# Per-tile stores in token order, float32 loads of the first tile on the SyncE queue, and decay tables from one position table, in a fused retention and top-k expert kernel

## The chip, the core and the metric

The kernel runs on one core of a Trainium2 chip. The metric is device time in microseconds (us). The engines are TensorE (PE for its matmuls, PEld for its weight loads), VectorE (DVE), ScalarE (ACT), GpSimd (POOL) and SyncE (SP). Each takes its instructions in the order in which the program issues them, and waits on semaphores for the others. DMA transfers are issued by POOL or by SP and run on 16 DMA engines.

## What is computed

Shapes are batch 4, heads 8, sequence 768, head width 64, all float32. First comes a linear attention with a decay per head, then a layer that passes the 128 highest-scored tokens of each batch through a two-layer network and adds the gated result to them; all other tokens keep the attention's output.

```python
gamma = 1.0 - 2.0 ** (-5.0 - np.arange(H))            # attention
for t in range(S):
    state = gamma * state + einsum('bhd,bhe->bhde', k[:, :, t], v[:, :, t])
    y[:, :, t] = scale * einsum('bhd,bhde->bhe', q[:, :, t], state)

x = y.transpose(0, 2, 1, 3).reshape(B, S, 512)        # experts
scores = einsum('bsd,d->bs', x, w_gate)
out = x.copy()
for b in range(B):
    top_idx = np.argpartition(-scores[b], capacity)[:capacity]    # 128 of 768
    ye = np.maximum(x[b, top_idx] @ w1, 0.0) @ w2                 # 512 -> 1024 -> 512
    g = 1.0 / (1.0 + np.exp(-scores[b, top_idx]))
    out[b, top_idx] = x[b, top_idx] + g[:, None] * ye
```

## The kernel before

**Tiles.** The sequence is cut into tiles of 256 tokens, three per batch, twelve in all (j = 0 to 11, batch j // 3). A partition of a loaded tile holds two consecutive tokens (r = 0, 1), so that a load moves runs of 128 elements per head (`tok`, line 294). Each tile is two chunks c of 128 tokens, and heads come in four pairs hp, or in two halves u. The loads of q, k and v (`load`, line 299) are issued by POOL, cast from float32 to bfloat16 on the way, and go to seven rotating buffers each. There are two loads of 128 KB for each tile and tensor, 72 in all; four more load w1 and four w2.

**The order.** All work is cut into small steps, and the string `ORDER` (line 32) is the order in which they are issued, over all engines at once. The number after a step is its tile, chunk or batch; a name such as S6 or P0 is the PSUM bank, or pair of banks, that it uses. Each engine works through its own steps in this order. The steps that matter here:

- `c_*`: constants. `c_iota*` write position tables on POOL; `c_small`, `c_mask`, `c_ident`, `c_late` and others work on DVE; `c_gq` and `c_gk` (lines 261 and 257) are exponentials on ACT that make the decay tables gq and gk for the three tile positions in a batch; `warm` (line 333) is four matmuls on zeros, which compute nothing that is used.
- `l_q`, `l_k`, `l_v`, `l_w1`, `l_w2`: the loads.
- `ks` (line 340): k times its decay table, on DVE. `tq` and `tk`: transposes of q and scaled k on PE. `eq` (times gq, on DVE) and `ek` (on ACT) bring them back from PSUM.
- `qk`, `mk`: products of q and k on PE, and the causal mask on DVE. `kv`, `se`: the state's update on PE, and its copy on ACT. `qs`, `av`: the output from the state and from the masked products.
- `ey` (line 430): the transposed output yT from PSUM, on ACT. `tx`, `ex`: it is transposed into rows and written to xs (bfloat16, all 24 chunks stay). `sp`, `esp`: the scores.
- `srt`, `esr`, `cp`, `cpi`, `dg`, `rk`, `oh`: for each batch the rank of each token by comparison with all others. Equal scores are told apart by the table `tie` on the diagonal blocks. `oh` is a one-hot matrix of the chosen. `spl`, `ga`, `ega`, `sig`: the chosen tokens' index and gate.
- `gx`, `egx`, `m1`, `rl`, `m2`, `cb`: chosen rows are gathered by a matmul, then the two layers and the gate.
- `st` (line 577): a store of rows to the output; `sca` (line 585): a scatter of the 128 results of a batch. For batches 0 to 2 the scatter adds to what the store has written; for batch 3 the row is gathered too (`gr`), added on chip (`cb`, line 562), and the scatter writes plainly. A scatter waits for the stores of its batch. Stores and scatters are issued by POOL, and between two of them POOL writes one element (`spaced`, line 572).

**Order of tokens.** Within a chunk of 128 tokens, the columns of yT, and so the partitions of xs, are ordered by r first and token pair second: partition 64 r + i is token 2 i + r. Each of the eight stores therefore takes one r of one batch: 64 partitions, six chunks, every second row of the output, 768 KB. The tables `lq` and `tie` hold this order.

**Start and end.** The order begins with the constants, eight `warm` steps between them (32 matmuls), and the loads of tile 0. It ends with

```python
"... st 3 1;gr 3 S6; st 3 0;rl 2 2 P1; ... m2 2 2 S6;egx 3 S5;m1 3 0 P0;cb 2 S6;m1 3 1 P0; ..."
"... sca 2;ga 3 S6; m2 3 0 S4;rl 3 1 P0;ega 3 S6;sig 3;m2 3 1 S4;cb 3 S4;sca 3;"
```

so that batch 3's scatter comes last.

Of the kernel before, what the change touches and what calls it, by code (L numbers as in the profile page):

```python
# [15 lines left out]
try:  # L16
# [13 lines left out]
NX = 7  # L30
EKD, EXD = [], []
ORDER = (
    "c_small;c_tab;l_v 0 1;l_wg;l_k 0 1;c_szero;c_iota;c_zero;warm S6;l_k 0 0;c_mask;c_gq 0;warm S6;c_slg;"
    "c_ident;l_k 1 1;warm S6;c_wg;l_k 1 0;warm S6;c_gk 2;c_iota2;warm S6;l_q 0 0;c_gk 1;l_q 0 1;warm S6;c_gq 1;"
    "l_q 1 0;warm S6;c_iota3;warm S6;l_v 0 0;c_late;c_gk 0;l_q 1 1;tq 0 0 S6;c_gq 2;l_v 1 1;eq 0 0 S6;l_k 2 0;"
    "ks 0 1;tq 0 1 S6;ks 0 0;tk 0 1 S0;l_k 2 1;ks 1 2;tk 0 0 S1;ek 0 1 S0;eq 0 1 S6;l_v 1 0;tk 1 2 S2;ek 0 0 S1;"
    "qk 0 1 P2;l_q 2 1;ek 1 2 S2;qk 0 0 P0;mk 0 1 P2;kv 0;l_v 2 1;tq 1 2 S6;se 0;mk 0 0 P0;l_v 3 0;kv 1;l_q 2 0;"
    "se 1;eq 1 2 S6;qs 0 P1;av 0 1 P1;l_v 2 0;av 0 0 P1;qk 1 0 P2;ks 2 2;l_k 4 0;ey 0 P1;qk 1 1 P0;mk 1 0 P2;"
    "tk 2 2 S6;l_k 3 1;kv 2;ek 2 2 S6;l_k 3 0;sp 0 S2;mk 1 1 P0;tx 0 S3;l_q 3 1;se 2;esp 0 S2;ex 0 S3;l_q 5 0;"
    "qs 1 P2;av 1 1 P2;l_k 4 1;kv 3;av 1 0 P2;l_q 3 0;se 3;tq 2 2 S6;ey 1 P2;kv 4;l_q 4 0;eq 2 2 S6;l_v 3 1;"  # L40
    "se 4;qk 2 0 P0;sp 1 S6;qk 2 1 P1;mk 2 0 P0;l_q 4 1;tx 1 S4;l_v 4 1;ex 1 S4;ks 3 2;qs 2 P0;l_v 5 0;"
    "av 2 0 P0;mk 2 1 P1;tk 3 2 S5;l_v 7 1;ek 3 2 S5;esp 1 S6;ks 4 2;av 2 1 P0;l_v 4 0;ey 2 P0;tq 3 2 S6;"
    "l_k 6 0;tk 4 2 S4;eq 3 2 S6;l_q 5 1;tx 2 S5;ek 4 2 S4;sp 2 S6;l_k 5 1;qk 3 0 P1;esp 2 S6;qk 3 1 P0;"
    "mk 3 0 P1;ex 2 S5;kv 6;l_k 5 0;tq 4 2 S6;spl 0;se 6;srt 0 6 P2;mk 3 1 P0;kv 7;esr 0 6 P2;l_k 9 1;qs 3 P1;"
    "eq 4 2 S6;av 3 1 P1;se 7;av 3 0 P1;cp 0 3;l_v 5 1;qk 4 1 P0;qk 4 0 P2;ey 3 P1;cp 0 5;kv 8;l_k 6 1;"
    "mk 4 1 P0;se 8;l_q 6 0;tx 3 S6;sp 3 S2;tq 5 2 S3;ex 3 S6;mk 4 0 P2;l_q 6 1;l_v 6 1;kv 9;eq 5 2 S3;qs 4 P0;"
    "se 9;l_v 6 0;av 4 1 P0;ks 5 2;av 4 0 P0;l_q 9 0;esp 3 S2;cp 0 4;ey 4 P0;tk 5 2 S6;l_k 8 1;kv 10;cp 0 0;"
    "ek 5 2 S6;cp 0 1;tx 4 S4;l_k 9 0;sp 4 S5;ks 6 2;ex 4 S4;l_q 8 0;qk 5 1 P1;qk 5 0 P0;esp 4 S5;cp 0 2;"
    "tk 6 2 S6;l_q 7 1;se 10;mk 5 0 P0;tq 6 2 S5;l_v 8 0;ek 6 2 S6;eq 6 2 S5;l_q 7 0;qs 5 P0;kv 12;mk 5 1 P1;"
    "l_k 7 0;qk 6 0 P2;se 12;av 5 0 P0;l_k 7 1;qk 6 1 P1;mk 6 0 P2;av 5 1 P0;l_q 9 1;kv 13;ey 5 P0;mk 6 1 P1;"  # L50
    "l_q 8 1;qs 6 P2;av 6 0 P2;se 13;sp 5 S6;l_k 8 0;tx 5 S0;ks 9 2;av 6 1 P2;l_q 11 0;ex 5 S0;esp 5 S6;"
    "dg 0 0 6;tk 9 2 S6;spl 1;srt 6 6 P1;ey 6 P2;tq 7 2 S1;l_v 7 0;rk 0 S0;ek 9 2 S6;eq 7 2 S1;l_q 10 0;ks 7 2;"
    "sp 6 S1;esr 6 6 P1;tx 6 S6;l_v 9 0;esp 6 S1;oh 0 S0;tq 9 2 S1;ex 6 S6;tk 7 2 S4;l_v 8 1;eq 9 2 S1;ga 0 S5;"
    "tq 8 2 S6;ek 7 2 S4;l_v 10 1;ega 0 S5;ks 8 2;gx 0 S5;l_k 11 0;sig 0;cp 1 2;l_v 10 0;eq 8 2 S6;qk 7 0 P1;"
    "tk 8 2 S4;l_v 9 1;cp 1 5;egx 0 S5;kv 14;mk 7 0 P1;ek 8 2 S4;l_q 10 1;qk 7 1 P0;l_k 10 1;se 14;mk 7 1 P0;"
    "qk 8 1 P2;qk 8 0 P1;l_w1 0;kv 15;qs 7 P0;mk 8 0 P1;l_k 10 0;se 15;av 7 1 P0;av 7 0 P0;l_v 11 0;kv 16;"
    "cp 1 1;ey 7 P0;qk 9 0 P1;l_w2 1;mk 8 1 P2;l_q 11 1;qk 9 1 P0;se 16;tx 7 S6;mk 9 1 P0;sp 7 S4;l_w1 1;"
    "tq 10 2 S5;ex 7 S6;l_k 11 1;kv 18;eq 10 2 S5;st 0 0;qs 8 P0;cp 1 0;l_w1 2;av 8 1 P0;mk 9 0 P1;se 18;"
    "av 8 0 P0;l_w1 3;ey 8 P0;kv 19;ks 10 2;l_v 11 1;qs 9 P1;av 9 1 P1;se 19;cp 1 3;sp 8 S6;st 1 0;av 9 0 P1;"
    "tx 8 S5;esp 8 S6;dg 1 0 6;l_w2 0;ey 9 P1;kv 20;l_w2 2;tk 10 2 S6;ex 8 S5;sp 9 S0;l_w2 3;tq 11 2 S1;cp 1 4;"  # L60
    "st 0 1;ek 10 2 S6;esp 9 S0;esp 7 S4;tx 9 S0;eq 11 2 S1;st 2 1;srt 12 6 P1;se 20;ks 11 2;st 2 0;qk 10 1 P2;"
    "ex 9 S0;srt 18 2 S6;mk 10 1 P2;rk 1 S1;spl 2;esr 12 6 P1;tk 11 2 S0;oh 1 S1;esr 18 2 S6;qk 10 0 P2;st 1 1;"
    "ek 11 2 S0;kv 21;cp 2 3;gx 1 S6;se 21;mk 10 0 P2;ga 1 S2;qk 11 1 P0;egx 1 S6;cpi 9;qs 10 P2;mk 11 1 P0;"
    "av 10 0 P2;av 10 1 P2;kv 22;ey 10 P2;ega 1 S2;m1 1 2 P0;cp 2 0;dg 2 0 6;sig 1;se 22;sp 10 S6;qk 11 0 P1;"
    "rl 1 2 P0;cp 2 4;tx 10 S4;esp 10 S6;mk 11 0 P1;srt 20 2 S6;ex 10 S4;m1 0 2 P0;cp 2 2;esr 20 2 S6;cp 2 1;"
    "qs 11 P1;cpi 10;rl 0 2 P0;av 11 1 P1;av 11 0 P1;m2 1 2 S6;ey 11 P1;dg 3 0 2;cp 2 5;dg 3 2 2;sp 11 S5;"
    "rk 2 S4;cb 1 S6;esp 11 S5;spl 3;srt 22 2 S6;m2 0 2 S5;oh 2 S4;esr 22 2 S6;dg 3 4 2;cpi 11;ga 2 S6;tx 11 S4;"
    "cb 0 S5;gx 2 S0;ex 11 S4;sca 0;ega 2 S6;rk 3 S1;egx 2 S0;sca 1;sig 2;m1 2 2 P1;oh 3 S1;st 3 1;gr 3 S6;"
    "st 3 0;rl 2 2 P1;gx 3 S5;egr 3 S6;m2 2 2 S6;egx 3 S5;m1 3 0 P0;cb 2 S6;m1 3 1 P0;rl 3 0 P0;sca 2;ga 3 S6;"
    "m2 3 0 S4;rl 3 1 P0;ega 3 S6;sig 3;m2 3 1 S4;cb 3 S4;sca 3;"  # L70
# [4 lines left out]
def kernel(  # L75
# [44 lines left out]
    VX = many(NX, [128, H, 2, D], BF, "vx")  # L120
    KP = many(3, [128, HP, 2, 2, D], BF, "kp")
# [32 lines left out]
    tq = sb.tile([128, NJ, 2, 2, 64], FT)  # L154
# [8 lines left out]
    biasc = sb.tile([128, 1], FT)  # L163
# [49 lines left out]
    def c_iota():  # L213
        nc.gpsimd.iota(spos, pattern=[[T, NJ], [0, H], [1, 2]], base=0, channel_multiplier=2,
                       allow_small_or_imprecise_dtypes=True)
        nc.gpsimd.iota(tq[:, 0], pattern=[[128, 2], [1, 2], [2, 64]], base=0, **iota)
        nc.gpsimd.iota(jp, pattern=[[1, 128]], base=0, channel_multiplier=-1)
        for s in range(2):
            nc.gpsimd.iota(loc[s * 64:(s + 1) * 64], pattern=[[1, 2]], base=0, channel_multiplier=2,
                           allow_small_or_imprecise_dtypes=True)  # L220

    def c_iota2():
        for jt in range(1, NJ):
            nc.gpsimd.iota(tq[:, jt], pattern=[[128, 2], [1, 2], [2, 64]], base=T * jt, **iota)
# [10 lines left out]
    def c_small():  # L235
# [5 lines left out]
        nc.vector.memset(biasc, math.log(scale))  # L241
# [52 lines left out]
    def tok(src, j, u):  # L294
        b, jt = divmod(j, NJ)
        return bass.AP(tensor=src.tensor, offset=src.offset + b * H * S * D + jt * T * D + u * 4 * S * D,
                       ap=[[2 * D, 128], [S * D, 4], [1, 2 * D]])

    def load(x, src, j, u):
        nc.gpsimd.dma_start(x[j % NX][:, 4 * u:4 * u + 4].rearrange("p h r d -> p h (r d)"), tok(src, j, u))  # L300

    def l_q(j, u):
        load(QX, q, j, u)

    def l_k(j, u):
        load(KX, k, j, u)
# [123 lines left out]
    def ey(j, bank):  # L430
        ac.activation(YT[j % 3].rearrange("p c h t -> p (c h t)"), PS[bank], AF.Copy)
# [153 lines left out]
    def sca(b):  # L585
# [13 lines left out]
    for entry in ORDER.split(";"):  # L599
        f = entry.split()  # L600
        if f:
# [3 lines left out]
            if f[0] in ("st", "sca", "l_q", "l_k", "l_v", "l_w1", "l_w2") or f[0] == "spl" and f[1] != "3":  # L605
# [36 lines left out]
```

## Time and profile before

| what | value |
|---|---|
| runs | 111.98, 112.34, 119.0 us |
| median | 112.34 us |
| profiled execution | 113.11 us |
| its span in the profile | 111.3 us |
| TensorE clock granted | 0.994 |
| PE busy | 94.5 us (85%), of it 9.4 on the warming matmuls |
| DVE, ACT, POOL busy | 78.5, 73.5, 77.2 us |
| moved by DMA | 19.16 MB, mean 172 GB/s |

The profile is of one execution. Its span is what the hardware profiler recorded; its own time, 113.11 us, is 1.8 us longer, and lies 0.77 us above the median. Matmuls are pipelined and their ends are modelled, so that a full PE is not PE at its peak. "issue" as the releaser of an idle time means that the engine waited for nothing that the profile shows. "L179" is a helper that records every operation, so lines with it are told apart by the tiles that they write and read.

### The profile page before, as it was taken

To read this page: it belongs to the slowest core of one execution; us is meant where nothing else is said; L and a number is where in the kernel's file an instruction comes from. 1 tells how busy PE (TensorE), PEld (TensorE's weight loads), DVE (VectorE), ACT (ScalarE), POOL (GpSimd) and SP (SyncE) were. 2 spreads that over 40 slices of the span, in tenths; PEclk is the share of its full clock that TensorE was granted. 3 is DMA by queue.
4 is the path that set the end of the run, shared out by engine and by line. 5 is a ranking of instruction groups with operands and counts; after the bars stand their busy time and mean duration, and the time that the engine had idled before them with its cause. 6 is when DMAs were issued, how large, how long until landed. Compare 5 with 4: busy or idle time off the path is not lost.

```text
span 111.3 us, 4553 instructions
## 1 busy us (share of the span) xinstructions
PE 94.5 (85%) x1970; PEld 72.7 (65%) x1974; DVE 78.5 (70%) x214; ACT 73.5 (66%) x117; POOL 77.2 (69%) x129
## 2 busy tenths in 40 slices
PE   0999798999899996999999899696956999999910
PEld 0334467777687874888977778585856777976600
DVE  5433379828779999998999989597865979600320
ACT  5599586985878887488995778774653745353300
POOL 6999999997989999989999666653600001970630
PEclk9999999999999999999999999999999999999997
DMA  0999999999999999999999999999999600399962
GB/s 1 94 123 125 134 138 170 173 179 178 180 168 142 138 144 156 180 182 141 161 141 165 158 184 263 287 295 249 287 399 418 168 14 0 27 130 365 247 85 94
DMA packets 43939, 19.16 MB, mean 172 GB/s; under 512 B 38864, under 2 KB 39888, under 8 KB 43920
## 3 DMA queue, kind: packets, MB, share of 16 engines
q0 software_dynamic: 43392, 18.88, 125.5%
q8 instruction: 15, 0.25, 0.8%
q1 hardware_dynamic: 528, 0.00, 0.2%
q14 instruction: 4, 0.03, 0.1%
HBM read 23.07 MB, written 7.34 MB: 273 GB/s over the span
## 4 chain that ended last, share of the span: by engine, by line
DMA 26%; PE 22%; issue 18%; POOL 13%; DVE 10%; ACT 6%; POOLq 1%; DVEq 0%; ACTq 0%
DMA out_dram<-xs 20%; PE pB L179 11%; PE pA L179 8%; DMA kx<-in_k_dram 6%; POOL vx L300 4%; POOL out_dram L587 3%; POOL qx L300 3%; PE pS L179 3%; DVE kp L179 2%; DVE g L179 2%; DVE am L179 2%; ACT sst L179 2%; ACT yT L179 2%; POOL kx L300 1%; DVE qT L179 1%
## 5 line engine op out<-in xcount | busy, mean ns | idle before, releaser
L179 DVE TENSOR_TENSOR am<-pA,mask 128x1024 bf16<-128x1024 f32 x24 | 28.5, 1215 | 5.1 <-PE pA L179 4.9
L300 POOL DMA_DIRECT2D vx<-in_v_dram x24 | 19.0, 799 | 1.7 <-POOLq L623 0.8
L587 POOL DMA_INDIRECT out_dram<-ot,idx x4 | 6.2, 1548 | 19.6 <-ACT ot L179 17.3
L300 POOL DMA_DIRECT2D kx<-in_k_dram x24 | 18.7, 795 | 0.4 <-DMA qx<-in_q_dram 0.4
L300 POOL DMA_DIRECT2D qx<-in_q_dram x24 | 18.7, 796 | 0.2 <-PE pA L179 0.2
L179 ACT ACTIVATE sst<-pS 64x256 bf16<-64x256 f32 x40 | 15.0, 375 | 5.7 <-PE pS L179 4.2
L179 PEld LDWEIGHTS <-kp 64*128 64x128 bf16 (+1 forms) x256 | 14.8, 95 | 4.5 <-DVE kp L179 0.8
L179 DVE TENSOR_SCALAR g<-wr,sc 128x256 bf16<-128x256 f32 (+4 forms) x44 | 16.6, 441 | 0.3 <-ACT wr L179 0.3
L179 ACT ACTIVATE yT<-pA 128x1024 bf16<-128x1024 f32 x12 | 12.3, 1022 | 2.7 <-PE pA L179 2.5
L179 PE MATMUL pS<-vx,kp 64*128 64x128 bf16 x160 | 12.5, 217 | 0.6 <-ACT sst L179 0.3
L179 ACT ACTIVATE xs<-pA 128x1024 bf16<-128x1024 bf16 x9 | 9.2, 1023 | 4.3 <-PE pA L179 4.3
L179 PE MATMUL pB<-zero 128*128 128x512 bf16 x32 | 9.4, 465 | 3.0 <-DVE zero L251 3.0
L179 PE MATMUL pA<-qT,kT 64*64 64x128 bf16 x384 | 9.2, 220 | 2.9 <-issue 2.1
L581 POOL DMA_DIRECT2D out_dram<-xs x8 | 6.3, 846 | 6.9 <-DVE am L179 1.6
L179 PEld LDWEIGHTS <-yT 128*128 128x128 bf16 x192 | 8.6, 97 | 2.0 <-ACT yT L179 0.7
L179 PEld LDWEIGHTS <-kT 64*64 64x64 bf16 x384 | 6.5, 106 | 4.5 <-issue 3.0
L179 DVE TENSOR_TENSOR kp<-kx,gk 128x512 bf16<-128x512 bf16 (+1 forms) x26 | 9.1, 395 | 0.3 <-DMA kx<-in_k_dram 0.3
L179 ACT ACTIVATE kT<-pA 128x1024 bf16<-128x1024 bf16 (+1 forms) x8 | 7.2, 916 | 3.0 <-PE pA L179 2.9
L179 PEld LDWEIGHTS <-zero 128*128 128x128 bf16 x32 | 3.6, 115 | 8.3 <-DVE zero L251 3.0
L179 PE MATMUL pA<-am,vx 64*64 64x128 bf16 x384 | 8.7, 220 | 0.3 <-DVE am L179 0.3
L179 PEld LDWEIGHTS <-qx 128*64 128x64 bf16 x192 | 5.9, 109 | 3.4 <-issue 2.7
L179 PE MATMUL pA<-xg,w 128*128 128x128 bf16 x128 | 7.8, 219 | 0.0
(95 smaller groups left out, 172.5 us busy)
## 6 DMA issues: line engine op xcount, KB each, us to landing
out_dram<-xs POOLq DMA_DIRECT2D x8, 768.0 KB, 10.4
vx<-in_v_dram POOLq DMA_DIRECT2D x24, 128.0 KB, 5.1
kx<-in_k_dram POOLq DMA_DIRECT2D x24, 128.0 KB, 5.0
qx<-in_q_dram POOLq DMA_DIRECT2D x24, 128.0 KB, 5.4
w<-in_moe_w_dram POOLq DMA_DIRECT2D x8, 256.0 KB, 9.4
out_dram<-ot,idx POOLq DMA_INDIRECT x4, 5.0
wgf<-in_moe_w_gate_dram SPq DMA_DIRECT2D x1, 2.0 KB, 2.1
```

The lines of the kernel that those rows point to most:

```text
L179: i = getattr(self.engine, name)(*a, **k)
L300: nc.gpsimd.dma_start(x[j % NX][:, 4 * u:4 * u + 4].rearrange("p h r d -> p h (r d)"), tok(src, j, u))
L581: i = nc.gpsimd.dma_start(o, xs[r * 64:(r + 1) * 64, b * NC:(b + 1) * NC, :])
L587: i = nc.gpsimd.indirect_dma_start(out=out_rows, out_offset=bass.IndirectOffsetOnAxis(ap=IDX[b][:, :1], axis=0), in_=OT[b % 2], in_offset= ...
```

## The change

1. **Stores.** `ey` writes yT with its columns in token order (i first, r second): it reads PSUM with a step of 64 float32 and writes consecutive elements. Partition p of xs is then token p of its chunk. `st` takes a tile instead of an r and a batch: 128 partitions, two chunks, 256 consecutive rows of the output, 512 KB, twelve stores for eight. `lq` becomes the partition number, and `tie` comes from the difference table `jp`.
2. **First loads.** q and k of tile 0 go as float32 into two new buffers QF and KF, in two halves each, issued by SP. A new step `cq` casts q to bfloat16 on DVE. `ks` of tile 0 reads KF directly. All other loads stay with POOL.
3. **Decay tables.** One table `tq` of positions in a tile takes the place of three. `c_gq` gets the tile's start from a bias per tile position and head pair (`biasc`), computed on DVE. `c_iota2` is gone.
4. **The order.** `ORDER` is a new one throughout. It has five `warm` steps, all after the first `tq`, and other places for most steps. At its end batch 2's second layer and scatter follow batch 3's.

```diff
 ORDER = (
-    "c_small;c_tab;l_v 0 1;l_wg;l_k 0 1;c_szero;c_iota;c_zero;warm S6;l_k 0 0;c_mask;c_gq 0;warm S6;c_slg;"
-    "c_ident;l_k 1 1;warm S6;c_wg;l_k 1 0;warm S6;c_gk 2;c_iota2;warm S6;l_q 0 0;c_gk 1;l_q 0 1;warm S6;c_gq 1;"
-    "l_q 1 0;warm S6;c_iota3;warm S6;l_v 0 0;c_late;c_gk 0;l_q 1 1;tq 0 0 S6;c_gq 2;l_v 1 1;eq 0 0 S6;l_k 2 0;"
...
+    "c_tab;c_iota;l_k 0 1;c_zero;l_wg;c_small;l_q 0 1;l_q 0 0;l_k 0 0;l_v 0 0;c_mask;c_gq 0;l_v 0 1;c_ident;"
+    "c_slg;c_szero;l_q 1 1;l_q 1 0;c_gk 1;l_k 1 1;cq 0 1;c_gq 1;c_wg;c_iota3;tq 0 1 S6;warm S0;l_k 1 0;l_v 1 0;"
+    "eq 0 1 S6;warm S1;cq 0 0;c_gk 0;c_late;l_k 2 0;tq 0 0 S6;warm S2;l_v 1 1;c_gq 2;warm S3;l_k 2 1;ks 0 0;"
+    "l_q 2 1;warm S4;eq 0 0 S6;ks 0 1;l_q 2 0;tk 0 0 S6;tq 1 2 S5;ek 0 0 S6;l_v 2 0;kv 0;eq 1 2 S5;tk 0 1 S6;"
+    "l_k 4 1;qk 0 0 P0;ek 0 1 S6;mk 0 0 P0;l_v 3 0;se 0;qk 0 1 P1;l_v 2 1;c_gk 2;kv 1;ks 1 2;qs 0 P2;l_k 3 0;"
...
+    "ex 5 S5;l_q 8 0;dg 0 0 6;qs 6 P1;av 6 1 P1;se 13;l_k 9 0;av 6 0 P1;ey 6 P1;st 2;tq 7 2 S5;ks 7 2;l_k 10 0;"
...
+    "mk 10 1 P0;sig 0;st 5;kv 20;st 8;tk 11 2 S2;oh 1 S6;tq 11 2 S3;se 20;st 4;qk 10 0 P0;ek 11 2 S2;eq 11 2 S3;"
+    "kv 21;st 1;gx 1 S6;mk 10 0 P0;ey 9 P2;st 7;dg 2 0 6;se 21;qs 10 P1;av 10 0 P1;egx 1 S6;av 10 1 P1;"
...
+    "m1 3 1 P0;rl 3 0 P0;ega 2 S3;ga 3 S6;m2 3 0 S4;rl 3 1 P0;ega 3 S6;egr 3 S2;m2 3 1 S4;sig 3;sig 2;m2 2 2 S6;"
+    "cb 3 S4;sca 3;cb 2 S6;sca 2;"
 )
...
+    KF = sb.tile([128, H, 2, D], FT)
+    QF = sb.tile([128, H, 2, D], FT)
...
-    def c_iota2():
-        for jt in range(1, NJ):
-            nc.gpsimd.iota(tq[:, jt], pattern=[[128, 2], [1, 2], [2, 64]], base=T * jt, **iota)
...
-        nc.vector.memset(biasc, math.log(scale))
+        for jt in range(NJ):
+            nc.vector.tensor_scalar(biasc[:, jt], lg, float(T * jt), math.log(scale), op0=OP.mult, op1=OP.add)
...
-            nc.scalar.activation(gq[:, jt, hp], tq[:, jt], AF.Exp, bias=biasc[:, 0:1], scale=lg[:, hp:hp + 1])
+            nc.scalar.activation(gq[:, jt, hp], tq, AF.Exp, bias=biasc[:, jt, hp:hp + 1], scale=lg[:, hp:hp + 1])
...
-        nc.vector.tensor_scalar(tie, tq[:, 0, 0].rearrange("p r i -> p (r i)"), lq[:, 0:1], 1.1754944e-38,
-                                op0=OP.is_gt, op1=OP.mult)
+        nc.vector.tensor_scalar(tie, jp, 0.0, 1.1754944e-38, op0=OP.is_gt, op1=OP.mult)
...
     def l_q(j, u):
-        load(QX, q, j, u)
+        if j:
+            load(QX, q, j, u)
+        else:
+            nc.sync.dma_start(QF[:, 4 * u:4 * u + 4].rearrange("p h r d -> p h (r d)"), tok(q, j, u))
...
+    def cq(j, u):
+        ve.tensor_copy(QX[j % NX][:, 4 * u:4 * u + 4], QF[:, 4 * u:4 * u + 4])
...
+            x = KX[j % NX] if j else KF
+            ve.tensor_mul(KP[j % 3][:, hs(u), r], x[:, h, r].rearrange("p (h s) d -> p h s d", s=2),
...
     def ey(j, bank):
-        ac.activation(YT[j % 3].rearrange("p c h t -> p (c h t)"), PS[bank], AF.Copy)
+        ac.activation(YT[j % 3].rearrange("p c h (i r) -> p (c h) i r", r=2),
+                      PS[bank].rearrange("p (g r i) -> p g i r", g=2 * HP, r=2), AF.Copy)
...
-    def st(b, r):
+    def st(j):
         spaced()
-        o = bass.AP(tensor=out.tensor, offset=out.offset + (b * S + r) * Dm,
-                    ap=[[2 * Dm, 64], [128 * Dm, NC], [1, Dm]])
-        i = nc.gpsimd.dma_start(o, xs[r * 64:(r + 1) * 64, b * NC:(b + 1) * NC, :])
+        b = j // NJ
+        o = bass.AP(tensor=out.tensor, offset=out.offset + j * T * Dm, ap=[[Dm, 128], [128 * Dm, 2], [1, Dm]])
+        i = nc.gpsimd.dma_start(o, xs[:, 2 * j:2 * j + 2, :])
```

## The prediction

> **What bounds the kernel now.** I read the busy time of each engine by stage first, then the timeline of the start, then the stretches where TensorE waits for nothing visible, and last the scatters that end the run.
>
> The stages (columns: stage in us, its length, then busy time of PE, PEld, DVE, ACT, POOL with instruction counts, granted clock, DMA share, GB/s):
>
> ```profile
> 12.30:34.50 22.20, 20.18 (x482) 15.97 (x482) 16.44 (x29) 16.55 (x27) 21.18 (x34) 1.00 1.72 168
> 34.50:66.10 31.60, 29.35 (x790) 24.51 (x788) 30.79 (x58) 25.04 (x41) 28.85 (x43) 1.00 1.55 157
> 66.10:84.40 18.30, 14.32 (x338) 12.19 (x339) 13.56 (x39) 11.70 (x20) 8.36 (x19) 1.00 1.39 299
> 84.40:97.20 12.80, 12.66 (x247) 10.48 (x249) 10.93 (x35) 6.72 (x10) 2.70 (x3) 1.00 0.42 105
> 97.20:106.10 8.90, 8.73 (x97) 5.99 (x96) 1.05 (x5) 3.59 (x6) 4.14 (x8) 1.00 1.08 236
> ```
>
> From 34.5 to 66.1 VectorE is busy 30.79 of 31.60 us: it sets the pace there, with PE close behind. Before, from 12.3 to 34.5, DVE idles 5.8 us and the tiles run at the pace of the chain transpose, product, mask, eviction. From 84.4 on PE is full (12.66 of 12.80, 8.73 of 8.90). Between 66.1 and 84.4 no engine is full. POOL is full to about 63 us, but its loads run some four tiles ahead (tile 9's loads are issued while tile 5 is worked on), and the waits hold only 0.3 us of DVE and none of PE for a load. So shorter POOL work gains nothing in the middle.
>
> The timeline of the start (start, length, engine):
>
> ```profile
> 3.05 9.37 PE L179 MATMUL pB<-zero 128*128 128x512 bf16 x32 [3.05 <-DVE zero L251]
> 7.72 4.20 PEld L179 LDWEIGHTS <-zero 128*128 128x128 bf16 x20 [0.28 <-issue]
> 12.35 0.41 PE L179 MATMUL pB<-ident,qx 128*64 128x128 bf16 x8
> ```
>
> The first transpose starts when the 32 warming matmuls end, not when its q lands: q's first half was issued at 7.31 and took 3.3 us, so it was there at 10.6. Until 7.72 these matmuls come every 0.43 us, after it every 0.21.
>
> PE waiting for nothing visible, late in the run:
>
> ```profile
> 70.58 0.63 PE L179 MATMUL pA<-ident,qx 128*64 128x128 bf16 x15 [1.07 <-issue]
> 77.06 0.79 PE L179 MATMUL pB<-oh,xs 128*128 128x128 bf16 x11 [0.84 <-issue]
> 84.37 0.35 PE L179 MATMUL pA<-qT,kT 64*64 64x128 bf16 x10 [2.07 <-issue]
> ```
>
> These 4.0 us fall where the stores and weights load the DMA engines most (299 GB/s in that stage, 403 GB/s in 82.2 to 84.5). DVE idles with them.
>
> The end, with the answer for the scatters' line (issue to landing over the four):
>
> ```profile
> 106.15 0.75 DVE L179 SCALAR_TENSOR_TENSOR ot<-pA,axf,XR 128x512 f32<-128x512 f32 x1 [1.39 <-PE pA L179]
> 107.18 1.01 POOL L587 DMA_INDIRECT out_dram<-ot,idx  x1 [2.03 <-DVE ot L179]
> ```
> ```profile
> L587 POOL DMA_INDIRECT out_dram<-ot,idx x4: 1012/1624/1932, 94.2 to 107.2; - x4
> ...
> DMA to landing us min/median/max: 2.8/5.0/5.1
> ```
>
> By windows the four are 5.1, 5.1, 4.9 and 2.8: the three that add onto the output take 5 us, beside stores or not; the last, for batch 3, writes plainly. The end follows at once: 107.18 + 2.8 = 110.0, then about 1.3 us of drains.
>
> **What the Trainium skill says.** "TensorE: Matmul & The Clock Gate", What's actually happening: a cold array runs at half clock and is released after a window of some 3.4 us of activity, free-running. The trace agrees: 0.43 then 0.21 us, after 4.7 us. "Runtime: NRT & Kernel Launch", Instruction fetch mechanics: instructions come by DMA in blocks of 256. The trace has 15 instruction packets on queue 8 for PE's 3944 instructions (15.4 blocks), which fits; that the late stalls are fetches behind stores is my reading. The page calls the fetch mostly hidden; the 2.07 us here does not agree. "DMA: Bandwidth & Descriptors", SWDGE vs HWDGE vs iDMA: a transfer that casts must come from GpSimd, one from SyncE does not cast; hence the casts on VectorE. Same page, Rules for kernel authors: an accumulating DMA reads its destination and writes it later, which fits 5 us against 2.8.
>
> **The change, part by part.**
>
> *Loads of tile 0 on SyncE.* Four of 72 loads leave POOL: 4 x 0.80 = 3.2 us less, plus two tq position tables and one lq, 0.9 us. Four more stores come in, at 0.69 us each, 2.7. POOL gains 1.4 us, worth nothing as said. SyncE's one transfer (the gate weights) costs 0.42 us to issue and lands in 2.1. With four half-tiles beside it, five issues end near 2.9; with about 0.75 us of data each (POOL's 128 KB of bf16, 256 KB read, follow each other every 0.76 us) q's halves land near 4.5 and 5.0, k by about 6. The first k and q would land up to 5 us earlier than now.
>
> *What then gates PE.* By the new order VectorE does, from 0.82: zero 0.27, memsets 1.0, three bias columns at 0.17 each (the row of 128x4 operations) 0.5, mask 0.74, ident 0.29, slg 0.35, state memsets 0.82, ones 0.06: to 4.85, and a cast of 128x512 (0.23 for 128 elements in the slots row, 0.42 for a qT of this size; I take 0.4): 5.3. PE: tq 0 1 cold 0.85 (twice 0.41); then two warming blocks, 8 x 0.43 = 3.4; tq 0 0 0.5; three blocks warm, 12 x 0.21 = 2.5: tk 0 0 starts at 12.6. Its operands are there near 10 (the gk table comes third on ScalarE, at 8.8: 2.65 for the bias, 2.08 + 1.04 + 2.08 + 1.04; then ks 0 0). So the warming blocks still stand in front of it. Now the first tk starts at 13.70: 1.1 us gained. From there PE's order tk, tq 1, kv, tk, qk gives 0.41 + 0.64 + 0.6 + 0.41 + 0.42: the first mask at 15.1 (now 15.80). Carrying the rows on (mask 1.22, eviction 1.02, kT 1.02, states 0.77, kp 0.75), tile 2's masks and tile 3's kp are done near 27.8, now at 28.35 (kp) and 28.37. **Gain 0.5 us**, bounded by 2.6 (tk at 10.0) and by a loss of 1 (a late window keeps PE cold 1 to 2 us longer).
>
> *DVE's additions.* Two casts 0.8, bias columns 0.4, four kp from float32 at about 0.1 more each: 1.6 us, all before 12 us, where DVE is busy 5 of 12 us; that idle time hides them. With less cover they would be paid once.
>
> *Decay tables.* 12 exponentials stay 12, at 0.59 us; bias comes per table and head pair instead of one column. No cost beyond the bias columns counted above.
>
> *ey in token order.* The same 1024 elements, but the read of PSUM steps 256 bytes. No row here shows such a read. The skill ("PSUM — Partial Sum Buffer", Specifications (TRN2)) says that 8-byte lines make non-contiguous patterns slow for matmuls, and "ScalarE: Activation LUTs", What ACT_TABLE_LOAD costs, has an ACTIVATE at one element per cycle whatever the function; from these, between nothing and double (12 x 1.02 = 12.3 us of ACT). I take nothing. A gain is excluded, the element count being the same.
>
> *Stores per tile.* 12 x 512 KB for 8 x 768 KB: the same 6.3 MB. Now they land in 6 to 12 us and nobody waits except POOL (1.3) and the last scatter, whose stores land at 105.45, before its operand (106.90). Smaller last stores gain nothing. Two start earlier (st 2, st 6), six still follow closely near tiles 9 and 10, with w2: the 4.0 us of stalls may become 1.5 or 6.5. I take 4.0.
>
> *The new order in the middle.* Same products; DVE's 31 us full stretch stays. I take 0, bounds -2 and +3.
>
> *The end.* Remaining PE work is the same, but m2 2 now comes after m2 3, so batch 2's scatter comes last. PE's last product ends as now (106.05); cb 2 on ACT is 0.69 (now 0.75 on DVE); POOL has sca 3 done by then. The last landing is then an adding one, 5.0 instead of 2.8: **+2.2 us**. Bounds: 0.5 (PE ends earlier) and 3 (POOL's issue 1.6 instead of 1.0, after a spacer of 0.6).
>
> **Sum.** The profiled execution took 113.11 (span 111.3): -0.5 + 2.2 = 114.8. It lies 0.77 above the median 112.34, so the median should be **114.0**.
>
> **Rivals.** *Start and stalls win*: PE reaches tk at 10.5 (2.1 more gained) and the spread stores leave 1.5 us of stalls (2.5 gained): 114.0 - 4.6 = 109.4. For it: the operands are there at 10, and two stores leave the crowded stage. Against it: five warming blocks in PE's own queue, and six stores in a row. *Slow token-order eviction (slower)*: ey is on the chain from the products to scores, output transposes and freed banks. ACT idles 30 of 94 us, so about half of what is added shows; from 0.35 us per ey (2.1 shown) it takes the result past 2%. Doubled: 6 us, 120; at half that, 117. Against it: one element per cycle whatever the function. *Crowded stores*: stalls of 6.5 us and a mid order 1 us worse: 117.5. *The loads do not arrive earlier in effect*: PE starts as now because of the warming, only the end changes: 114.5, inside the likeliest case.
>
> **Numbers.** Likeliest case (nearly level start, longer last landing) 0.5, own range 112.3 to 115.6; start and stalls win 0.17; slow eviction 0.13; crowded stores 0.2. Two per cent, about what a measurement of this kernel tells from no change, is 110.1 to 114.6. Faster: the first rival less its weaker half, 0.15. Slower: a quarter of the likeliest, the two slow rivals: 0.42. The rest, 0.43, within. The range 110.2 to 117.6 leaves out most of the first rival and the doubled eviction.
>
> **What would show it.** The first tk near 12.6 and warming between 5.3 and then; q landed by 5; tile 2's last mask near 27; ey at 1.02 us (1.4 and up: the second rival); PE's "issue" waits after 60 us summed near 4; the last DMA an adding scatter landing 5 us after issue. If tk starts near 10, or the stalls vanish, the prediction is too high; if ey is long, or DVE idles between 34 and 66 us, too low.

## The result and the profile after

The changed kernel takes 117.88 us (median of four executions, 116.88 to 118.81), the kernel before, run beside it, 112.19. The ratio is 1.048, with a 95% interval from 1.039 to 1.057: slower by 5.4 us at that ratio (112.19 times 0.048). The profiled execution took 118.38 us with a span of 116.6, against 113.11 and 111.3 before. The 5.3 us between the spans are read below. A ratio compares only the executions within 1.5% of the fastest of their kernel (here 117.38 for 112.04 us at the median); medians and ranges are of all executions, and stand alone where the record has no ratio.

The answer by stages for the changed kernel (stage, its length, busy time of PE, PEld, DVE, ACT and POOL with instruction counts, granted clock, DMA share, GB/s), from 12.30 to the last product:

```profile
12.30:34.50 22.20, 20.38 (x504) 15.91 (x501) 15.70 (x25) 17.14 (x28) 21.70 (x31) 1.00 1.80 180
34.50:50.00 15.50, 13.22 (x350) 10.59 (x346) 13.84 (x27) 12.05 (x19) 13.92 (x19) 1.00 1.72 188
50.00:58.50 8.50, 7.95 (x145) 7.01 (x134) 5.61 (x16) 3.77 (x4) 3.47 (x8) 0.60 1.12 182
58.50:84.40 25.90, 22.38 (x573) 18.67 (x572) 21.28 (x48) 18.99 (x30) 17.72 (x37) 1.00 1.32 237
84.40:97.20 12.80, 12.80 (x235) 10.27 (x233) 11.78 (x35) 6.98 (x13) 3.37 (x6) 1.00 0.47 116
97.20:108.20 11.00, 10.93 (x156) 8.07 (x153) 3.92 (x14) 4.52 (x9) 2.95 (x5) 1.00 0.46 90
```

The same 8.5 us in the kernel before:

```profile
50.00:58.50 8.50, 8.29 (x220) 7.10 (x221) 8.05 (x20) 8.01 (x11) 8.26 (x14) 1.00 1.55 150
```

PE is as busy there as before (7.95 and 8.29 us) but does 145 matmuls for 220: the granted clock is 0.60 on the mean, 0.50 from 52 to 58. VectorE, which set the pace of this stretch before (8.05 of 8.50), now waits for PE (5.61). Over all six rows PE is busy 87.66 us of 95.90; over the same work before it was 85.24 of 93.80. So PE reaches its last product 2.1 us later (108.13 for 106.05), with 2.4 more busy and 0.3 less idle: longer matmuls, not new waits.

The timeline of the start (start, length, engine; in brackets the idle time before it and what ended it):

```profile
5.80 0.48 DVE L181 CAST qx<-QF 128x512 bf16<-128x512 f32 x1 [2.06 <-DMA QF<-in_q_dram]
6.34 0.64 PE L181 MATMUL pB<-ident,qx 128*64 128x128 bf16 x8 [6.34 <-DVE qx L181]
6.91 3.59 PE L181 MATMUL pA<-zero 128*128 128x512 bf16 x8
10.43 0.51 PE L181 MATMUL pB<-ident,qx 128*64 128x128 bf16 x8
10.88 2.76 PE L181 MATMUL pA<-zero 128*128 128x512 bf16 x12
13.48 0.39 PE L181 MATMUL pB<-ident,kp 128*128 128x128 bf16 x4
15.71 1.23 DVE L181 TENSOR_TENSOR am<-pA,mask 128x1024 bf16<-128x1024 f32 x1 [0.55 <-PE pA L181]
```

The first transpose of q comes 6 us earlier than before (6.34 for 12.35), and none of it is left at the first mask: 15.71 for 15.80. Between them stand two warming blocks at half rate (8 matmuls in 3.59 us) and three more (12 in 2.76).

PE's longer waits for nothing visible, from 46 us on:

```profile
49.78 0.41 PE L181 MATMUL pA<-am,vx 64*64 64x128 bf16 x15 [0.73 <-issue]
75.67 0.86 PE L181 MATMUL pB<-ones,g 128*128 128x1 bf16 x29 [0.47 <-issue]
82.14 0.49 PE L181 MATMUL pA<-am,vx 64*64 64x128 bf16 x21 [0.86 <-issue]
```

After 60 us they sum to 1.6 us (a wait of 0.22 at 69.48 with them), for 4.0 before. The first of these three stands at the edge of the slow stretch: from 49 to 52 us PE is busy 1.71 of 3.00 us, and then the clock is at half.

The end, and the answer for the scatters' line:

```profile
108.22 0.69 ACT L181 ACTIVATE ot<-pB,axf 128x512 f32<-128x512 f32 x1 [2.34 <-issue]
108.74 0.09 POOL L583 MEMSET spacer<- 1x1 f32 x1
109.18 1.57 POOL L595 DMA_INDIRECT out_dram<-ot,idx  x1 [0.35 <-ACT ot L181]
```
```profile
L595 POOL DMA_INDIRECT out_dram<-ot,idx x4: 1016/1586/1720, 94.1 to 109.2; - x4
...
DMA to landing us min/median/max: 2.8/4.8/5.0
```

By windows the last one, which adds, takes 4.8: it lands at 114.0. The span ends 2.6 us after that; before it ended 1.3 after the landing at 110.0. From the last product to the end of the span there are 8.5 us, 5.25 before. Of these 3.2 us more, some 2.0 are the landing and 1.2 to 1.3 lie after it. With the 2.1 us of PE this is the whole of the 5.3.

And the evictions of yT, whose reading order the change turns:

```profile
L181 ACT ACTIVATE yT<-pA x12: 1018/1023/1024, 20.2 to 88.9; 128x1024 bf16<-128x1024 f32 x12
```

1023 ns at the median, as before the change.

### The profile page after: what moved, and what is told of

Its sections match the earlier page's. It is cut to its first block, busy times and chain, and to the rows that moved or that the text cites. A ratio compares the mean times of both kernels' runs of the same rounds, so it can differ in the third digit from the quotient of the medians.

```text
span 116.6 us, 4536 instructions
## 1 busy us (share of the span) xinstructions
PE 93.6 (80%) x1962; PEld 73.0 (63%) x1962; DVE 79.6 (68%) x218; ACT 73.5 (63%) x117; POOL 76.9 (66%) x129
## 4 chain that ended last, share of the span: by engine, by line
PE 62%; ACT 12%; issue 11%; DMA 6%; POOLq 2%; DVE 1%; POOL 1%; SPq 1%; ACTq 0%
PE pA L181 42%; PE pB L181 13%; PE pS L181 7%; ACT yT L181 4%; DMA QF<-in_q_dram 3%; ACT sst L181 3%; ACT kT L181 2%; DMA out_dram<-xs 2%; POOLq L645 2%; ACT xg L181 1%; POOL out_dram L595 1%; ACT xs L181 1%; DVE qT L181 1%; ACT ot L181 0%; SPq L277 0%
## 5 line engine op out<-in xcount | busy, mean ns | idle before, releaser
L589 POOL DMA_DIRECT2D out_dram<-xs x12 | 8.7, 722 | 16.4 <-ACT wr L181 8.2
L296 POOL DMA_DIRECT2D kx<-in_k_dram x22 | 17.5, 799 | 0.9 <-issue 0.3
L296 POOL DMA_DIRECT2D qx<-in_q_dram x22 | 17.1, 796 | 0.1
L181 DVE TENSOR_SCALAR g<-wr,sc 128x256 bf16<-128x256 f32 (+4 forms) x44 | 15.9, 415 | 0.8 <-ACT wr L181 0.8
L181 ACT ACTIVATE yT<-pA 128x1024 bf16<-128x1024 f32 x12 | 12.3, 1022 | 4.7 <-PE pA L181 4.4
L181 PE MATMUL pS<-vx,kp 64*128 64x128 bf16 x160 | 12.3, 217 | 0.4 <-ACT sst L181 0.2
L181 PE MATMUL pA<-am,vx 64*64 64x128 bf16 x384 | 9.5, 220 | 2.1 <-issue 2.1
L181 ACT ACTIVATE kT<-pB 128x1024 bf16<-128x1024 bf16 (+1 forms) x8 | 7.3, 916 | 5.6 <-PE pB L181 5.5
L181 ACT ACTIVATE xs<-pA 128x1024 bf16<-128x1024 bf16 x10 | 10.2, 1022 | 0.9 <-PE pA L181 0.6
L181 DVE TENSOR_TENSOR qT<-pA,gq 128x1024 bf16<-128x1024 bf16 x10 | 6.9, 685 | 5.2 <-PE pA L181 5.2
L181 PEld LDWEIGHTS <-vx 64*64 64x64 bf16 x384 | 6.2, 106 | 3.8 <-issue 2.4
L181 DVE TENSOR_TENSOR kp<-kx,gk 128x512 bf16<-128x512 bf16 x22 | 8.3, 417 | 0.0
```

The source lines that it names most:

```text
L181: i = getattr(self.engine, name)(*a, **k)
L296: nc.gpsimd.dma_start(x[j % NX][:, h].rearrange("p h r d -> p h (r d)"), tok(src, j, u))
L589: i = nc.gpsimd.dma_start(o, xs[:, 2 * j:2 * j + 2, :])
```

## The experiments

Theory at the outset: the end (an adding scatter last) and PE's slow stretch make the loss. Rival: the parts themselves (loads by SyncE, casts, twelve stores, turned eviction) do.

**The changed kernel with the plain scatter last.** Batch 2's second layer, gate and scatter go ahead of batch 3's (`e1_plain_last`):

```diff
-rl 2 2 P2;m1 3 0 P0;m1 3 1 P0;rl 3 0 P0;ega 2 S3;ga 3 S6;m2 3 0 S4;
...
-m2 3 1 S4;sig 3;sig 2;m2 2 2 S6;cb 3 S4;sca 3;cb 2 S6;sca 2
+rl 2 2 P2;ega 2 S3;sig 2;m2 2 2 S5;m1 3 0 P0;cb 2 S5;m1 3 1 P0;rl 3 0 P0;sca 2;ga 3 S6;m2 3 0 S4;
...
+m2 3 1 S4;sig 3;cb 3 S4;sca 3
```

> The changed kernel with batch 2's second layer, gate and adding scatter put back ahead of batch 3's second layer, so that the plainly writing scatter ends the run. If the last scatter's kind sets the end: 2.0 us less from its last product to landing (4.8 against 2.8) and about 1.3 us less in POOL's closing drain, so 114.0 to 115.0 us; the clock drop at 51 us stays. If the end is only late because all work before it is late: no change, 117 to 118 us.

Measured: 116.9 us (115.95 to 118.8), ratio 1.045 [1.036, 1.054]. Two lines of its timeline:

```profile
87.34 0.55 PE L180 MATMUL pA<-xg,w 128*128 128x128 bf16 x7 [2.87 <-issue]
109.83 0.99 POOL L594 DMA_INDIRECT out_dram<-ot,idx  x1 [1.94 <-DVE ot L180]
```

The last product ends at 108.70, the scatter lands 2.7 to 2.8 us after 109.83, and the span ends at 115.2: 6.5 us for 8.5. The end gives back its 2.0 us; the further 1.3 us expected don't come back, as 2.6 us still follow the landing. The time hardly follows, because PE now waits 2.87 us at 87.34 and the clock is at half from 28.0 to 31.5 us (0.74 on the mean from 28.0 to 34.5). The size of the end is shown; that it is the whole loss is refuted.

**The kernel before with the adding scatter last** (`e2_before_adding_last`), the same exchange from the other side:

```diff
-m2 2 2 S6;egx 3 S5;m1 3 0 P0;cb 2 S6;m1 3 1 P0;rl 3 0 P0;sca 2;ga 3 S6;
...
-m2 3 1 S4;cb 3 S4;sca 3;
+egx 3 S5;egr 3 S6;m1 3 0 P0;m1 3 1 P0;rl 3 0 P0;ga 3 S6;
...
+m2 3 1 S4;m2 2 2 S6;cb 3 S4;sca 3;cb 2 S6;sca 2;
```

> The kernel before with its last steps in the other order: batch 2's second layer and adding scatter after batch 3's. If the last scatter's kind sets the end: 3.3 us more, 115.5 us, and the last landing 5 us after its issue. If it is hidden: 112.2 us, as before.

Measured: 116.16 us (114.83 to 116.75) for 111.43, ratio 1.046 [1.040, 1.053].

```profile
105.46 1.04 POOL L586 DMA_INDIRECT out_dram<-ot,idx  x1 [6.92 <-DMA out_dram<-xs]
106.81 1.64 POOL L586 DMA_INDIRECT out_dram<-ot,idx  x1 [0.21 <-issue]
```

PE is done at 104.98, 1.1 us earlier than before; the adding scatter, held behind the plain one, lands 4.9 us after 106.81, at 111.7, and the span ends 1.4 later, at 113.1. From the last product that is 8.1 us, 2.9 more than before. The direction is confirmed. The medians differ by 4.7 us, more than this profile, which is of the lowest execution (114.83), shows; what makes up the rest isn't seen in a trace. The other five executions have lower mean clocks, 0.967 to 0.983 for 0.985, so part of it is probably the clock.

**Filling the gap before the slow stretch.** One more warming block in the changed kernel (`e3_fill_gap`):

```diff
-tq 7 2 S5;ks 7 2;l_k 10 0;sp 6 S0
+tq 7 2 S5;warm S1;ks 7 2;l_k 10 0;sp 6 S0
```

> The changed kernel with one more warming step (four matmuls on zeros, 0.85 us) between the transposes of q of tile 7 and the scores of tile 6, where TensorE waits 0.55 us for the eviction. If TensorE's idle time around 49 to 51 us lets its clock fall to half: the clock stays at 0.99 and the time falls by 2 to 3 us, to 115 us. If the clock falls for another reason, or the gap filled is too small: a mean clock of 0.96 to 0.97 again and 117 to 118 us.

Measured: 119.3 us (117.67 to 120.28). From 50.0 to 58.5 the clock stays at 1.00, and the time is not better:

```profile
86.31 1.33 PE L180 MATMUL pA<-xg,w 128*128 128x128 bf16 x11 [3.03 <-issue]
```

The clock then is at half from 86.0 to 89.4 (0.72 on the mean from 84 to 90). So the slow stretch is no fixed cost of one place. That the block held the clock up at 52 isn't proven either, as the next yardstick shows.

**The changed kernel once more** (`e5_after_again`), unedited, beside three others:

> The changed kernel unaltered, as a yardstick on this chip and to see whether the clock drop and the long TensorE waits of its first profile come again at the same places. If both follow from the order alone: the drop to half clock at 51 us again, 117 to 118 us. If they follow from when an instruction fetch happens to land among DMA traffic: similar time, but the drop and the long waits elsewhere.

Measured: 118.25 us (116.08 to 120.37) for 112.3. The profile is of the lowest execution:

```profile
84.93 0.55 PE L180 MATMUL pA<-xg,w 128*128 128x128 bf16 x7 [1.77 <-issue]
106.87 1.57 POOL L594 DMA_INDIRECT out_dram<-ot,idx  x1 [0.35 <-ACT ot L180]
```

No fall of the clock before the last product, other waits (1.28 at 43.88, 0.86 at 77.91, 1.77 here), the last product at 105.82, and again 8.5 us to the end. So in this execution the new order reaches its last product 0.2 us ahead of the kernel before (106.05), and the end alone makes the loss (spans 114.3 and 111.3). (The profile here is of the lowest of four executions; that of before lies 0.77 us above its median.) The end is constant; the slow stretches and long waits move from execution to execution.

**All parts, in the order of before** (`e4_parts_old_order`). The code is the changed one; the order is the old one, with the casts, with twelve stores in the places of eight, and with SyncE's loads first:

```diff
-c_wg;l_k 1 0;
+c_wg;cq 0 0;cq 0 1;l_k 1 0;
...
-st 0 0;
+st 0;st 1;
...
-st 3 0;
+st 11;
```

> The changed steps (float32 loads of tile 0 by SyncE with casts, one position table, token order, stores per tile) in the order of the kernel before: its eight warming steps, its places for all steps, its end; the twelve stores stand where the eight stood. If the new order makes the loss: 112 us, within 1 us of before, ScalarE's evictions of yT at 1.02 us. If one of the parts costs time: 114 us or more.

Measured: 112.83 us (112.56 to 113.34) for 111.43, ratio 1.014 [1.008, 1.021].

```profile
105.39 1.02 POOL L594 DMA_INDIRECT out_dram<-ot,idx  x1 [2.27 <-DVE ot L180]
```

It lands at 108.2, and the span ends at 110.8, 2.6 us after it, as in the changed kernel. The time lies between the two expectations. So parts alone cost 1.4%, some 1.6 us, and the order the other 3.3%. The rival is refuted as the main cause.

**Which part closes late.** The two halves of the code alone, in before's order: SyncE's float32 loads with the casts (`e6_loads_only`), and the token order with twelve stores (`e7_stores_only`).

```diff
-        load(QX, q, j, u)
+        if j:
+            load(QX, q, j, u)
+        else:
+            nc.sync.dma_start(QF[:, 4 * u:4 * u + 4].rearrange("p h r d -> p h (r d)"), tok(q, j, u))
```
```diff
-    def st(b, r):
+    def st(j):
```

The first edit is made for k likewise; with the second go the turned `ey`, `lq` and `tie`.

> The kernel before with q and k of tile 0 loaded as float32 by SyncE and cast, all else as before. The parts in the old order ended 1.2 to 1.3 us later after their last landing than before (2.6 us against 1.3). If the loads through SyncE cause that: 2.5 us from last landing to the end, about 1 per cent over before. If the stores cause it: 1.3 us and the time of before.

> The kernel before with token order and twelve stores by tile, loads and tables as before. If the stores cause the later end: 2.5 us from last landing to the end and about 1 per cent over before. If the loads cause it: 1.3 us and the time of before, with the last stores landing in about 4 us in place of 7.

Measured: with the loads 115.31 us (112.48 to 119.56) for 112.3; with the stores 112.19 (111.25 to 113.66), ratio 1.002 [0.997, 1.008]. The last scatter with the loads, then with the stores:

```profile
108.52 1.01 POOL L597 DMA_INDIRECT out_dram<-ot,idx  x1 [2.22 <-DVE ot L180]
```
```profile
105.50 1.02 POOL L584 DMA_INDIRECT out_dram<-ot,idx  x1 [2.00 <-DVE ot L178]
```

Both land 2.8 us later. With the loads the span ends at 113.8, 2.5 us after the landing; with the stores at 109.7, 1.4 after. Only the ends are read here: the profile with the loads (115.55 us) also holds a stretch at half clock, 83.9 to 87.3. Every kernel here whose first loads go by SyncE ends 2.0 to 2.6 us after its last landing (seven profiles), every one without them 1.3 to 1.5 (seven). What grows is a DRAIN, the instruction with which POOL closes the program. Before, then in the changed kernel (the last duration is the closing one, in ns):

```profile
L637 POOLq DRAIN  x3: 51/98/3630, 106.9 to 111.1; - x3
```
```profile
L645 POOLq DRAIN  x3: 51/103/6856, 108.9 to 116.3; - x3
```

It starts just ahead of the scatter's issue and ends at 110.6 before, 0.6 us after the landing, and at 115.8 in the changed kernel, 1.8 us after it. Why it lasts longer isn't shown. The stores, the turned eviction and the table for equal scores cost nothing that the ratio shows.

**The changed kernel without its stores** (`e8_no_stores`): all `st` steps are left out, so the rows that no scatter reaches aren't written.

```diff
-av 6 0 P1;ey 6 P1;st 2;tq 7 2 S5;
+av 6 0 P1;ey 6 P1;tq 7 2 S5;
```

> The changed kernel without its twelve stores, so that rows outside the 512 chosen are not written and the scatters add to what is there. If traffic of the stores delays TensorE's instructions and with that lets its clock drop: no wait of TensorE for nothing visible over 0.6 us after 45 us, clock 0.98 or more, TensorE done 3 us earlier, 113.5 to 114.5 us. If the order itself starves TensorE: 116 us or more and a drop of the clock again.

Measured: 115.69 us (113.51 to 117.39), against 118.25 (116.08 to 120.37) for the changed kernel beside it; the two lowest are 113.51 and 114.8 against 116.08 and 117.25. Its longest wait of PE for nothing visible:

```profile
44.14 0.33 PE L179 MATMUL pA<-ident,kp 128*128 128x128 bf16 x3 [1.01 <-issue]
```

After 55 us none reaches 0.2; with stores they went up to 1.77 (and 3.03 with the gap filled). The last product ends at 103.71, the earliest of the new order, and the clock falls only after it (mean 0.976). So in this one profile the late waits go with the stores. The one at 44.14 lies ahead of the first store's place (47.0 in the changed kernel) and stays. What exactly PE waits for isn't visible.

**The new order with the plain scatter last and all loads on POOL** (`e9_plain_last_pool`), both known costs of the end taken out. The order's end is that of the first experiment, and:

```diff
-            nc.sync.dma_start(QF[:, 4 * u:4 * u + 4].rearrange("p h r d -> p h (r d)"), tok(q, j, u))
+        load(QX, q, j, u)
```

> The changed kernel with two of its parts undone: the first tile is loaded by POOL as before, and batch 3's plain scatter ends the run; token order, stores per tile, one position table and the new order stay. If the later end makes most of the loss: from TensorE's last product to the end 5.3 us (8.5 in the changed kernel), and 113.5 to 115 us, the rest being waits for instructions and clock drops. If the new order itself makes it: 116 us or more with TensorE done at 108 us or later.

Measured: 115.36 us (113.19 to 116.89) for 112.82. The profiled execution (115.56) ends 5.4 us after its last product at 108.40, as the kernel before does (5.25); yet PE waits 2.87 us at 85.49 again, and the clock is at half from 86.0 to 89.5. Its close is 1.5 us, against 2.6 in the first experiment, from which it differs only in these loads and their casts. With the end mended the order is still not better than before's: its best execution, 113.19, lies above the three best of the kernel before beside it (110.42 to 112.04).

**An earlier start that doesn't wait for warming blocks** (`e10_early_start`). Before's order and end, twelve stores, one position table, POOL's loads. Only the head is new: q and k of tile 0 are loaded first, and four warming blocks stand ahead of the first transpose instead of eight.

```diff
+c_tab;c_iota;c_zero;warm S6;c_small;l_q 0 0;warm S6;c_gq 0;c_mask;l_k 0 1;
...
+tq 0 0 S6;l_v 0 0;eq 0 0 S6;l_q 1 0;ks 0 1;tq 0 1 S3;
...
+warm S4;c_gq 1 2;tk 0 0 S1;l_k 2 0;
```

> The order of the kernel before behind a new beginning, with token order, stores per tile, one position table and loads by POOL: position tables and zeros first, then q and k of tile 0, the decay tables of tile 0 first on ScalarE, and four warming steps ahead of the first transpose in place of eight. If warming and table order hold the start back: first transpose near 7 us in place of 12.3, tile 1's output near 20.5 us in place of 24, and 109 us, 3 us under before. If loads hold it: tile 2 waits for its k and q, and 111 to 112 us.

Measured: 114.54 us (112.43 to 117.55), ratio 1.016 [0.993, 1.038]. By stages (columns as above):

```profile
8.00:12.00 4.00, 2.35 (x25) 1.30 (x24) 2.18 (x8) 2.17 (x4) 3.94 (x8) 1.00 1.54 145
12.00:16.00 4.00, 4.00 (x75) 3.09 (x72) 2.95 (x3) 3.21 (x5) 4.00 (x7) 0.66 1.73 172
16.00:20.00 4.00, 4.00 (x88) 3.40 (x87) 3.05 (x5) 3.94 (x7) 4.00 (x7) 0.50 1.81 178
20.00:24.00 4.00, 4.00 (x72) 3.35 (x71) 1.39 (x18) 2.52 (x6) 4.00 (x6) 0.56 1.81 178
```

The first mask is at 12.79, three us earlier than before. Then PE, busy only 2.35 of 4.00 us from 8 to 12, runs at half clock from 13.3 to 23.5, and the second yT is evicted at 24.37 (24.00 before). The lead is gone within two tiles. But the fall isn't all: the profiled execution took 114.88 us, and the lowest, 112.43, with a mean clock of 0.996 and so without such a stretch, is no faster than the three best of the kernel before beside it (110.42 to 112.04).

**The same with more warming in the gap:** one more block (`e11_early_warm`), or three (`e12_early_warm3`).

```diff
-tk 0 0 S1;l_k 2 0;
+tk 0 0 S1;warm S4;l_k 2 0;
```
```diff
-tq 0 1 S3;l_q 1 1;
+tq 0 1 S3;warm S4;l_q 1 1;
...
-tk 0 0 S1;l_k 2 0;
+tk 0 0 S1;warm S4;warm S4;l_k 2 0;
```

> The early start (e10_early_start) again, with one more warming block (4 matmuls, about 0.85 us at full clock) where TensorE had nothing to do, after the second transpose of k, at 10.2 to 11.5 us. Theory A (TensorE's clock fell to half from 13 to 22 us in e10 because TensorE had been sparse from 8 to 12 us, and that ate the early start): with the gap filled the clock stays at full from 8 to 24 us, the second evicted tile starts near 21.5 instead of 24.4, and the lead of some 3 us at the first mask lasts at least to tile 2; the end 109 to 111 us if nothing else of the early part sets the pace. Rival B (the loads through GpSimd set the pace of the first tiles, the clock only fills what would be waiting): the clock stays up, but VectorE and TensorE wait for loads of tiles 1 and 2 and tile 2's eviction is at 28.5 or later, the end 111.5 to 113 us. Rival C (one block isn't enough): the clock falls again, 112.5 to 115 us.

> As e11_early_warm with three more warming blocks instead of one: two after the second transpose of k, one between the second transpose of q and the first of k; some 0.8 us later first masks than in e10 (near 13.5), TensorE nearly full from 7 to 24 us. Theory A: the clock holds at full even if one block left it falling in e11, second eviction near 22, end 109.5 to 111.5 us. Rival B: the clock holds and tile 2's eviction is still at 28.5 or later, end 111.5 to 113 us. Rival C (the fall has nothing to do with how sparse TensorE is): the clock falls here too, 112.5 to 115 us.

Measured: one block 110.7 us (110.0 to 113.04) for 112.77, ratio 0.984 [0.977, 0.992]; three blocks 114.15 (109.21 to 118.7). One block, by stages:

```profile
8.00:12.00 4.00, 2.81 (x18) 1.30 (x19) 2.24 (x8) 2.17 (x4) 3.94 (x8) 1.00 1.57 152
12.00:16.00 4.00, 3.89 (x114) 3.12 (x118) 2.95 (x3) 3.26 (x6) 4.00 (x7) 1.00 1.75 173
20.00:24.00 4.00, 2.81 (x68) 2.27 (x69) 1.25 (x15) 3.52 (x7) 4.00 (x6) 1.00 1.82 178
```

Three blocks, by stages:

```profile
8.00:12.00 4.00, 3.92 (x31) 2.18 (x32) 1.14 (x5) 2.17 (x4) 3.94 (x8) 1.00 1.63 156
20.00:24.00 4.00, 2.50 (x51) 1.83 (x48) 1.27 (x19) 3.15 (x6) 4.00 (x6) 0.81 1.79 176
24.00:28.00 4.00, 4.00 (x78) 3.21 (x71) 1.98 (x3) 2.20 (x5) 3.37 (x6) 0.50 1.81 179
```

With one block the clock holds in the profiled execution, and the evictions lead before's by 1.5, 0.7, 0.7 and 1.0 us in the first four tiles, 1.2 in the eighth. The lead at the first mask (3 us) doesn't last as theory A wanted: in both kernels PE stands 1.50 us from about 19.6 or 20.4 on, for a copy of the state by ACT, which has 2.2 us of late decay tables in front of it. Placing these later wasn't tried. At that same wait the clock falls in the three-block profile and holds in the one-block one, though the three blocks fill 8 to 12 better (3.92 for 2.81). So a filled gap isn't enough, and two of the one-block kernel's six executions still have mean clocks of 0.947 and 0.955. With three blocks 20 of 22 have 0.969 or less; the one with 0.997 is the lowest of all kernels here, 109.21.

The traces say more about when the clock falls. In each of the fourteen profiles the granted clock changes only at whole multiples of 3.41 us from its first rise. That grid lies elsewhere in each execution: the first rise is at 10.7 and at 9.8 us in the two profiles of the changed kernel. Seven falls come before the last product, and each closes a grid window in which PE was busy 2.13 us or less. Of the 382 such windows at full clock only 12 are so sparse; none of the other 370 is followed by a fall. Two pairs of equal waits show it. The wait of 1.50 us lies whole in one window with three blocks (first line, then the clock falls) and is split over two with one block:

```profile
19.10:22.51 3.41, 1.70 (x40) 1.36 (x40) 2.17 (x19) 3.37 (x7) 3.41 (x5) 1.00 1.77 178
```
```profile
16.62:20.03 3.41, 2.39 (x36) 1.81 (x36) 3.41 (x14) 3.38 (x6) 3.41 (x6) 1.00 1.79 177
20.03:23.44 3.41, 2.34 (x63) 1.87 (x64) 0.66 (x11) 2.93 (x7) 3.41 (x6) 1.00 1.82 179
```

So does the wait of 2.87 us, whole in `e9_plain_last_pool` (the clock falls) and split in `e1_plain_last` (it holds):

```profile
82.63:86.05 3.42, 0.56 (x11) 0.56 (x10) 3.42 (x14) 0.00 (x0) 0.34 (x2) 1.00 1.34 371
```
```profile
82.66:86.08 3.42, 1.81 (x41) 1.60 (x39) 3.41 (x10) 1.42 (x5) 1.61 (x4) 1.00 1.47 411
86.08:89.49 3.41, 2.15 (x59) 1.96 (x59) 2.05 (x8) 1.56 (x2) 0.00 (x0) 1.00 0.91 250
```

In the changed kernel the window ahead of the fall is 48.22 to 51.64, with PE busy 2.13 us; in the early start it is 9.85 to 13.27, with 2.00. So the rival that the fall has nothing to do with how sparse PE is doesn't fit the traces; theory A fits, if one counts by these windows. A sparse window doesn't suffice: between 1.70 and 2.13 us busy, five were followed by a fall and five not.

Of the 3.2 us by which the one-block profile (span 108.2) is shorter than before's, 1.2 are there at the eighth eviction; the later rest goes with shorter waits of PE (0.97, 1.01 and 0.21 after 60 us, for 4.0). The one-block version is the only one here whose ratio lies under 1, by 1.6% against the kernel before; two of its six executions, at 112.87 and 113.04, don't show the gain.

## Where the prediction was right and where it was wrong

The median, 117.88, lies 3.9 us above the forecast and 0.3 above the top of its range; the 117.38 that the ratio rests on lies 3.4 above the forecast and just inside. Slower was held nearly as likely as no change, and its chance of 0.42 is a little under what its own parts give (0.125, 0.13 and 0.2, together 0.455). By its steps:

- **The end, +2.2.** The mechanism was right: an adding scatter last, landing in 4.8 us instead of 2.8, shown from both sides by the exchanged orders. The term was too small. It measured +3.2, because the close after the landing was carried over as 1.3 us and became 2.6. The loads by SyncE bring that (loads alone 2.5, stores alone 1.4; 2.6 and 1.5 in the new order with and without them). The prediction priced these loads at the head of the kernel alone.
- **The start, −0.5.** It measured −0.1 at the first mask and −0.3 at the third eviction. q's half was cast at 5.80 instead of 5.3, the first tk came at 13.3 to 13.5 instead of 12.6. The reason was the forecast one, the warming blocks in PE's own queue.
- **Stalls, 4.0 (bounds 1.5 and 6.5).** 1.6 us in the profiled execution, 2.9 in its repetition, 3.4 with the plain scatter last (0.55 and 2.87). The bounds held. That they come with the stores, part of the reading given, is borne out by the one profile without stores; that they are instruction fetches isn't shown, and so neither is the disagreement with the page on fetches.
- **The middle, 0 (bounds −2 and +3).** This is the term that failed most, though not in every execution. In the profiled one the last product is 2.1 us later although start and stalls gave some back: PE is 2.4 us longer busy, with a stretch at half clock that the profile of before doesn't have. In the repetition, without such a stretch, it is 0.2 us earlier. With the 0.3 and 2.4 us that start and stalls gave back, counted as the prediction counts them, the middle cost 4.8 us in the profiled execution, over the bound of +3. The prediction asked only of the start, not of the rearranged middle, whether PE could lose its clock. "TensorE: Matmul & The Clock Gate", Why this matters for your kernels, in the Trainium skill, advises against idle gaps of PE above some 3 us. Here no gap near 50 us is over 0.73 us, and the clock fell. The measurement decides: not only a long gap but a window of 3.41 us with PE busy 2.13 us was followed by half clock, though not every window as sparse was.
- **Eviction in token order, 0 (bounds 0 and +12.3).** Right: 1023 ns in both, and no loss in the stores alone. The slow-eviction rival, which gave 117 to 120, is dead although its figure is near.
- **Stores per tile, casts, tables, 0.** Right for the stores: 1.002 [0.997, 1.008]. The casts weren't measured apart from the loads.

Of the rivals, crowded stores gave 117.5 by stalls of 6.5 us; the stalls were shorter, not longer. That the range reaches up to about the measured time is therefore luck: its upper part was there for longer stalls and slower evictions, and neither came. Of the 4.8% the parts make 1.4 (some 1.6 us, mostly the late close) and the order 3.3 (some 3.7 us), of which 2.0 us are the adding scatter. About 1.7 us are left for the clock and for PE's waits. This last figure is a difference, not measured alone.

What stays open: what PE waits for in these waits, what decides over the clock in windows with 1.70 to 2.13 us of work, and why POOL's closing DRAIN lasts longer after loads by SyncE.

## What to carry to other kernels

Price what ends the program as its own stage: the last transfer's kind, its latency and what follows its landing; here an adding scatter in place of a plain one and four loads moved to SyncE's queue cost 3.2 us of 112. A load that lands earlier is worth nothing while a block of other work stands in front of its consumer in the same engine's queue, so ask of each start what that engine still has queued. When an order is rearranged, look at the granted clock by stages before explaining anything by waits, and repeat the profile: what moves from one execution to the next isn't a property of a place.

## What the hardware showed that was not expected

- The close of the program depends on loads issued in its first 3.4 us: 2.0 to 2.6 us from last landing to the end with four loads of 256 KB by SyncE, 1.3 to 1.5 when only the gate weights go that way. The difference lies in POOL's closing DRAIN.
- TensorE's granted clock fell to 0.50 in a kernel whose longest gap nearby was 0.73 us. The seven falls before a last product lasted 3.4 us (four), 6.8 us (two) and 10.2 us (the early start): once, twice and three times the 3.41 us on whose grid every change of the clock lies. No window of that grid with PE busy over 2.13 us was followed by a fall.
- PE's waits for nothing visible reach 3.03 us in the new order with its stores; in the profile without any store none after 55 us reaches 0.2.
- ScalarE's eviction of 128x1024 float32 from PSUM takes 1023 ns whether it reads in order or with a step of 256 bytes.
